# Two steps' products with the values in one run on TensorE, the second maxima group behind a slice of filler

## The chip, the cores and the metric

The kernel runs on one core of one Trainium2 chip. The metric is the device time of one launch in microseconds (us). A kernel is timed several times and the median is taken. Times in the profile come from one profiled execution and count from the first instruction of the program.

## The reference

Two kinds of layer alternate, each with a residual: attention with 16 query heads that share one key and one value head, and a gated feed-forward layer. The pair is applied twice with the same weights.

```python
def _A_ref(x, wq, wk, wv, wo):            # S = 2048, D = 448, H = 16, Dh = 28
    q = (x @ wq).reshape(B, S, H, Dh).transpose(0, 2, 1, 3)
    k = x @ wk
    v = x @ wv
    scores = jnp.einsum("bhqd,bkd->bhqk", q, k) * (Dh ** -0.5)
    p = _softmax(scores, axis=-1)
    o = jnp.einsum("bhqk,bkd->bhqd", p, v)
    return o.transpose(0, 2, 1, 3).reshape(B, S, H * Dh) @ wo

def _B_ref(x, w_gate, w_up, w_down):      # F = 1792
    h = _sigmoid(x @ w_gate) * (x @ w_up)
    return h @ w_down

x = x + _A_ref(_layernorm(x), ...); x = x + _B_ref(_layernorm(x), ...)
x = x + _A_ref(_layernorm(x), ...); x = x + _B_ref(_layernorm(x), ...)
```

## The kernel before, in words

The order of all instructions is written out by the program itself: the tile framework adds semaphores, and what Python emits first stands first in an engine's queue.

**Units and steps.** The 2048 queries are cut into 16 units of 128 rows, the keys into 16 tiles of 128. A unit takes 16 steps, one for each key tile, so a layer has 256 steps. A step has these parts, each with a letter in the order string:

- S, four times: `scores` multiplies one key tile with the queries of four heads (`s`, L508, one full-array fp16 product with 96 rows, 512 columns). ScalarE then writes the exponentials into a tile `P` (L511). The `P` tiles turn through 8 buffers.
- P: `pv` multiplies four `P` tiles with the values (L519), four fp32 products side by side on four column strips of the array, added up over a unit in one PSUM bank `pv`. In the trace an fp32 product has two records, so one step shows 8. `pv` is called one step late: after the four scores of step n stands the product of step n-1 (`PLAG = 1`, list `PQ`).
- M: `group(mx)` runs one group of maxima for the next unit: four products on four row strips (`mx`, L466, 32 rows each), each reduced to a maximum by VectorE (L470, `mp`). With the largest score of each row known ahead, the exponentials need no second pass. `m` is half a group (two products).
- T: `finish()`. When the last group of a unit is done, VectorE joins the maxima (`m`, L485 and L486), and `finish` transposes them on TensorE (`mt`, L491), copies them (`mr`, L493) and has SyncE write them into a row of the next unit's query tile (`QS<-mr`, L494). The scores of that unit read this row.
- X: bookkeeping of the step: side work such as layer norms, loads and the small `kv` products is emitted when it is due (`tick`).
- F: a slice of filler: products of the feed-forward layer (`gp`, `up` at L346, `dn` at L706), of the output projection (`wo`, L615) or of the next queries (`qp`, L346), for as many ns as the rate says. At each slice the put-off evictions of filler are emitted too (`th`, `h` on ScalarE, `th`, `h` on VectorE, L669 to L681).

A pattern holds two steps. `FULL` is taken while the filler left makes over 600 ns a step, `LEAN` otherwise; `LEAN` splits each maxima group into two halves. A unit with filler is one that runs in `FULL`.

```python
while step < U * KT:
    order = FULL if rate > LEANR else LEAN
    for o in order:
        ...
        elif o == "P":
            if len(PQ) > (sn % 4 == 0) * PLAG:
                pv(*PQ.pop(0))
        ...
        else:
            fill.slice(rate * 2 / order.count("F"))
```

**Banks.** One PSUM bank belongs to `pv`. The other seven are one pool that `s`, `mx`, `gp`, `up`, `dn`, `qp`, `wo`, `kv` and `mt` share. Which bank a product gets is fixed when the program is written out, and the product waits for the engine that last reads what the bank held.

Of the kernel before, what the change touches and what calls it, by code (L numbers as in the profile page):

```python
# [8 lines left out]
F32 = mybir.dt.float32  # L9
# [10 lines left out]
def interleaved_layers_kernel(ctx: ExitStack, tc: tile.TileContext, x, wq, wk, wv, wo, wg, wu, wd, out, layers=2):  # L20
# [6 lines left out]
    nc = tc.nc  # L27
# [3 lines left out]
    NT, NB, G, KT, FC = S // 128, S // 512, H // 4, S // 128, F // 128  # L31
    U = NT
    TB, WB, HB = 2, 4, 10
    NBL = NT // TB
    EPS = 1e-5

# [5 lines left out]
    wk1 = ctx.enter_context(tc.tile_pool(name="wk1", bufs=2))  # L42
# [27 lines left out]
    def flush(every=False):  # L70
        todo, pend[:] = pend[:], []
        for i, (due, fn) in enumerate(todo):
            if due > now[0] and not every:
                pend.append((due, fn))
            else:
                fn()
        if every and pend:
            flush(True)
# [331 lines left out]
    def qgen(l, b):  # L410

        XT = XTQ.pop((l, b))
        for g in range(G):
            yield from qproj(l, XT, b, g)
        flush(True)
# [89 lines left out]
    def scores(l, u, kt, g, P):  # L505
        assert ("m", l, u) in stored, (l, u, kt)
        s = psf.tile([128, 512], F32, tag=BANKS["s"], name="s", bufs=NBK[BANKS["s"]])
        nc.tensor.matmul(s, KK[l][0:96, 0, kt * 128:(kt + 1) * 128], QS[l, u][:, g].rearrange("p h n -> p (h n)"),  # L508
                         start=True, stop=True)
        p = wk1.tile([128, 512], F32, tag="P", name="P", bufs=8)  # L510
        nc.scalar.activation(p, s, AF.Exp, scale=esc)  # L511
        P.append(p)

    def pv(l, u, kt, P):
        if kt == 0:
            PVS[l, u] = psv.tile([128, 512], F32, tag="v", name="pv")
        v = PVS[l, u]
        for g in range(4):
            nc.tensor.matmul(v[32 * g:32 * g + 32], VV[l][:, kt], P[g], start=kt == 0, stop=kt == KT - 1,  # L519
                             tile_position=(0, 32 * g))  # L520
        if kt == KT - 1:
            o = wk1.tile([128, 512], F32, name="pvs", bufs=1)
            nc.scalar.copy(o, v)
            PVS[l, u] = o
# [5 lines left out]
    def later(*stages):  # L530

        side.append([stages[0][0], list(stages)])

    def tick():

        for s in list(side):
            s[0] -= 1
            if s[0] <= 0:
                flush()
                fill.run(s[1].pop(0)[1]())  # L540
                if s[1]:
                    s[0] = s[1][0][0]
                else:
                    side.remove(s)

    class Block:
# [8 lines left out]
        def tile(self, u):  # L555
# [84 lines left out]
            def ff():  # L640
                self.fed += 1
                if self.fed == TB:
                    fill.add(self.bulk(), BULK)
                    if b == NBL - 1 and not self.last:
                        fill.add(qgen(l + 1, 1), G * QCH)
# [372 lines left out]
    for b, g in sorted(qnew):  # L1018
        fill.add(qrest(b, g), QCH)

    FULL = "FSFSFSFSTPXMFSFSFSFSTPXM"
    LEAN = "FSFSmFSFSTPXmFSFSmFSFSTPXm"
    PLAG = 1
    LEANR = 600.0
    MORE = (5, 10)
    FIRST = KT * TB + 16
# [2 lines left out]
    for l in range(layers):  # L1029
# [15 lines left out]
        P = []  # L1045
        sn = 0
# [3 lines that stand above are left out]
                u, kt = divmod(step, KT)  # L1050
                if o == "S":
                    su, skt = divmod(sn // 4, KT)
                    if sn < 4 * U * KT:
                        scores(l, su, skt, sn % 4, P)
                        sn += 1
                        if sn % 4 == 0:
                            PQ.append((l, su, skt, P))
                            P = []
# [6 lines left out]
# [3 lines that stand above are left out]
                elif o == "X":  # L1068
# [9 lines left out]
                    tick()  # L1078
                    fed = sum(BLK[l, b].fed == TB for b in range(NBL) if (l, b) in BLK)
                    if fed < NBL - 1:  # L1080
                        rate = fill.left / max(FIRST + TB * KT * fed - step, 1)
# [7 lines left out]
        flush(True)  # L1089
        later(*BLK[l, NBL - 1].tile(U - 1))  # L1090
        if not final:
# [33 lines left out]
```

## Time and profile before

| what | value |
|---|---|
| median of 3 runs | 2327.27 us (2326.44 to 2330.89) |
| the profiled execution | 2331.67 us, span 2329.9 us |
| mean granted TensorE clock | 0.988 |
| TensorE busy | 96% of the span |
| VectorE busy | 70% |
| ScalarE busy | 67% |
| share of the span on TensorE in the chain that ended last | 53% |

The profiled execution is 4.4 us above the median of the runs. In the profile PE is TensorE's matmuls, PEld its weight loads, DVE VectorE, ACT ScalarE, POOL GpSimd, SPq the queue of SyncE, which issues most DMAs. A row of the timeline gives the start in us, the time from the first start to the last end, engine, line, operation, output and inputs, shape, and how many instructions were merged; in brackets stands the idle time of the engine before it and what ended it. Matmul records overlap, since they are pipelined: what a product costs the queue is the distance from its start to the start of the next row, not its own duration.

### The profile page before, as it was taken

The page shows a single profiled execution, that of the slowest core. Times are in us where ns is not written, and L with a number is a line of the kernel's source. Part 1 is how long each engine was busy: PE and PEld are TensorE (multiplying, and loading weights), DVE is VectorE, ACT ScalarE, POOL GpSimd, SP SyncE. Part 2 cuts the span into 40 slices and gives each one's busy share as a digit, 9 for nine tenths or more (in the row PEclk, how much of TensorE's full clock was granted, in tenths as well). Part 3 has the DMA queues.
Part 4 walks back from the last instruction along what each step waited for, and adds up shares of the span by engine and source line. Part 5 has one row for each costly group of instructions (what it writes and reads, how often), then busy time and mean ns, then how long its engine had stood idle before and what let it go on. Part 6 is the DMA issues. An engine that isn't in the chain of part 4 may idle for free.

```text
span 2329.9 us, 41129 instructions
## 1 busy us (share of the span) xinstructions
PE 2246.5 (96%) x15770; PEld 1003.9 (43%) x15770; DVE 1637.6 (70%) x2887; ACT 1552.1 (67%) x2573; POOL 331.4 (14%) x599
## 2 busy tenths in 40 slices
PE   4899999999999999999999999999999999999999
PEld 3312244444444444444562224444444444444456
DVE  5888887777777777773358887767777777777322
ACT  4577886777667677777413877767676767767751
POOL 6345351000110000001101010000000000000010
PEclk9989999999999999999998999999999999999999
DMA  5624552323223232322341112323131313223133
GB/s 145 202 92 125 173 157 71 97 77 95 92 68 101 70 90 75 95 93 80 97 139 53 28 50 93 89 83 87 60 99 59 99 59 99 77 83 95 59 113 118
DMA packets 224693, 217.53 MB, mean 93 GB/s; under 512 B 154656, under 2 KB 185568, under 8 KB 224496
## 3 DMA queue, kind: packets, MB, share of 16 engines
q1 hardware_dynamic: 218784, 199.12, 29.5%
q0 software_dynamic: 3552, 12.12, 1.3%
q10 hardware_dynamic: 2160, 3.67, 0.5%
q8 instruction: 123, 2.02, 0.4%
q14 instruction: 74, 0.61, 0.1%
HBM read 175.37 MB, written 23.59 MB: 85 GB/s over the span
## 4 chain that ended last, share of the span: by engine, by line
PE 53%; DVE 3%; DMA 1%; ACT 1%; issue 1%; POOL 0%; SPq 0%; ACTq 0%; POOLq 0%; DVEq 0%
PE pv L519 12%; PE s L508 11%; PE gp L346 7%; PE dn L706 7%; PE up L346 7%; PE mx L466 5%; DVE mp L470 2%; PE wo L615 2%; PE qp L346 1%; ACT P L511 1%; DMA sums<-rc 0%; PE mt L491 0%; DMA rc<-sums 0%; DVE m L485 0%; DMA sums<-pvs 0%
## 5 line engine op out<-in xcount | busy, mean ns | idle before, releaser
L511 ACT ACTIVATE P<-s,esc 128x512 f32<-128x512 f32 x2048 | 1303.6, 689 | 489.7 <-PE s L508 473.0
L470 DVE TENSOR_REDUCE mp<-mx 128x1 f32<-128x512 f32 x2048 | 1269.2, 683 | 381.5 <-PE mx L466 380.0
L508 PE MATMUL s<-QS,KK 96*128 96x512 f16 x2048 | 747.7, 383 | 19.0 <-ACT P L511 9.5
L346 PEld LDWEIGHTS <-wgu 128*128 128x128 f16 x4928 | 458.6, 97 | 237.0 <-issue 91.5
L519 PE MATMUL pv<-P,VV 128*32 128x512 f32 x4096 | 551.4, 610 | 0.0
L346 PE MATMUL up<-XT,wgu 128*128 128x256 f16 x2464 | 374.6, 272 | 0.0
L346 PE MATMUL gp<-XT,wgu 128*128 128x256 f16 x2464 | 374.2, 273 | 0.2 <-DVE mp L470 0.2
L706 PE MATMUL dn<-WD,h 128*128 128x448 f16 x1344 | 321.4, 352 | 0.0
L466 PE MATMUL mx<-KK,QH 32*128 32x512 f16 x2048 | 255.5, 389 | 13.5 <-DMA QH<-qd 4.0
L466 PEld LDWEIGHTS <-QH 32*128 32x128 f16 x2048 | 62.0, 91 | 462.3 <-issue 457.1
L508 PEld LDWEIGHTS <-KK 96*128 96x128 f16 x2048 | 189.5, 97 | 131.0 <-issue 57.8
L706 PEld LDWEIGHTS <-h 128*128 128x128 f16 x1344 | 124.1, 98 | 137.8 <-issue 24.0
L593 POOL TENSOR_TENSOR lb<-pvs,lb 128x512 f32<-128x512 f32 x32 | 40.7, 1270 | 968.3 <-DMA lb<-sums 812.7
L519 PEld LDWEIGHTS pv<-P,VV 128*32 128x32 f32 x4096 | 81.5, 108 | 185.8 <-issue 174.3
L680 ACT ACTIVATE h<-th 128x512 f16<-128x512 f32 x112 | 70.4, 628 | 84.0 <-DVE th L677 83.8
L677 DVE SCALAR_TENSOR_TENSOR th<-th,up 128x512 f32<-128x512 f32 x112 | 76.1, 680 | 58.8 <-PE up L346 46.2
L681 DVE SCALAR_TENSOR_TENSOR h<-th,h 128x512 f16<-128x512 f32 x112 | 77.9, 695 | 46.8 <-ACT h L680 46.8
L669 ACT ACTIVATE th<-gp,gsc 128x512 f32<-128x512 f32 x112 | 76.9, 687 | 47.9 <-PE gp L346 47.9
L306 POOL TENSOR_SCALAR rs<-mv 128x1 f32<-128x1 f32 (+2 forms) x53 | 12.2, 230 | 640.2 <-DVE mv L301 581.1
L346 PE MATMUL qp<-XT,WQ 128*128 128x512 f16 x352 | 98.8, 392 | 1.0 <-DVE mp L470 0.7
L615 PE MATMUL wo<-WO,oT 128*128 128x448 f16 x384 | 79.4, 357 | 0.2 <-DVE oT L600 0.2
L346 PEld LDWEIGHTS <-WQ 128*128 128x128 f16 x352 | 32.9, 100 | 51.9 <-issue 26.7
(138 smaller groups left out, 803.8 us busy)
## 6 DMA issues: line engine op xcount, KB each, us to landing
wgu<-wgu_d SPq DMA_DIRECT2D x224, 512.0 KB
QS<-qd SPq DMA_DIRECT2D x384, 32.0 KB
lb<-sums SPq DMA_DIRECT2D x128, 64.0 KB
wgu_d<-sgu POOLq DMA_DIRECT2D x14, 512.0 KB, 3.5
qd<-qst POOLq DMA_DIRECT2D x18, 256.0 KB, 2.7
xr<-in_A_x_dram SPq DMA_DIRECT2D x16, 224.0 KB
QH<-qd SPq DMA_DIRECT2D x28, 128.0 KB
x2d<-x SPq DMA_DIRECT2D x16, 224.0 KB
```

The source lines that it names most:

```text
L346: nc.tensor.matmul(ps, a, b, start=n == 0, stop=n == 10)
L466: nc.tensor.matmul(ps[h], qh[32 * h:32 * h + 32, g], KK[l][32 * h:32 * h + 32, 1, kb * 512:(kb + 1) * 512], start=True, stop=True, tile_po ...
L470: nc.vector.tensor_reduce(mp[:, g, h, kb:kb + 1], ps[h], axis=AX.X, op=OP.max)
L508: nc.tensor.matmul(s, KK[l][0:96, 0, kt * 128:(kt + 1) * 128], QS[l, u][:, g].rearrange("p h n -> p (h n)"), start=True, stop=True)
L511: nc.scalar.activation(p, s, AF.Exp, scale=esc)
L519: nc.tensor.matmul(v[32 * g:32 * g + 32], VV[l][:, kt], P[g], start=kt == 0, stop=kt == KT - 1, tile_position=(0, 32 * g))
L615: nc.tensor.matmul(p, v["oT"][:, a, h * 128:(h + 1) * 128], WO[:, c, h], start=n == 0, stop=n == 11)
L669: defer(lambda: nc.scalar.activation(th, gp.rearrange("p j n -> p (j n)"), AF.Tanh, scale=gsc))
L677: nc.vector.scalar_tensor_tensor(t, th, 1.0, up.rearrange("p j n -> p (j n)"), op0=OP.add, op1=OP.mult)
L680: nc.scalar.activation(h[:, 0], t, AF.Copy, scale=2.0 ** -17)
L681: defer(lambda: nc.vector.scalar_tensor_tensor(h[:, 1], t, 2.0 ** -17, h[:, 0], op0=OP.mult, op1=OP.subtract), 1)
L706: nc.tensor.matmul(p, hs[f // 2][:, a, o:o + 128], WD[:, f, c], start=n == 0, stop=n == 3 * FC - 1)
```

## The change

The string `FULL` is written anew. In its first step two `P` stand together, the second step has none; the second step has no `T`; and the second step's `M` stands behind one more slice of filler instead of behind a `P`. So a pattern has nine slices in place of eight, each 8/9 as long. In the steady state three sets of `P` tiles are there when the two `pv` come (those of steps n-2, n-1 and n), so the `P` tiles turn through 12 buffers in place of 8. Room for them is made by a smaller scratch area for the descriptors of GpSimd's DMAs (4096 bytes of each partition; it is the default otherwise).

```diff
     TB, WB, HB = 2, 4, 10
+    PB = 12
...
-        p = wk1.tile([128, 512], F32, tag="P", name="P", bufs=8)
+        p = wk1.tile([128, 512], F32, tag="P", name="P", bufs=PB)
...
-    FULL = "FSFSFSFSTPXMFSFSFSFSTPXM"
+    FULL = "FSFSFSFSTPPXMFSFSFSFSFXM"
     LEAN = "FSFSmFSFSTPXmFSFSmFSFSTPXm"
     PLAG = 1
+
...
-    nc = _bacc.Bacc("TRN2", target_bir_lowering=False, num_devices=1)
+    nc = _bacc.Bacc("TRN2", target_bir_lowering=False, num_devices=1, dynamic_dma_scratch_size=4096)
```

Line numbers behind the first edit are one higher in the changed kernel, and two higher behind the string.

TensorE's order where a unit's maxima are transposed, in the second layer's part where `dn` is the filler. Before, in the second step of a pattern:

```order
L508 MATMUL s<-QS,KK 128x512
L491 LDWEIGHTS m_20722
L491 MATMUL mt<-id_79,m_20722 16x128
L519 MATMUL pv<-P,VV 32x512 x4
L466 LDWEIGHTS QH
L466 MATMUL mx<-KK,QH 128x512
```

Now the same transpose of the same unit, in the first step of a pattern:

```order
L509 MATMUL s<-QS,KK 128x512
L492 LDWEIGHTS m_20721
L492 MATMUL mt<-id_79,m_20721 16x128
L520 MATMUL pv<-P,VV 32x512 x8
L467 LDWEIGHTS QH
L467 MATMUL mx<-KK,QH 128x512
```

The run of products with the values has grown from four to eight, and the transpose has moved four scores products further down.

TensorE's order at a maxima group in the same stretch. Before, every group stands right behind products with the values:

```order
L508 LDWEIGHTS KK
L508 MATMUL s<-QS,KK 128x512
L519 MATMUL pv<-P,VV 32x512 x4
L466 LDWEIGHTS QH
L466 MATMUL mx<-KK,QH 128x512
```

Now the group of the second step, between two slices of filler:

```order
L509 MATMUL s<-QS,KK 128x512
L707 LDWEIGHTS h
L707 MATMUL dn<-WD,h 128x448
...
L467 LDWEIGHTS QH
L467 MATMUL mx<-KK,QH 128x512
...
L707 LDWEIGHTS h
L707 MATMUL dn<-WD,h 128x448
```

In front of the group there is no product with the values any more, but two or three of the filler. Over the whole program the products with the values stand in 508 runs of four and 2 of eight before, and in 94 runs of four and 209 of eight now. Of the maxima groups of four, 369 stood behind products with the values before and 190 do now; 179 more stand behind filler.

## The prediction

> **What bounds the kernel now.** I read the page from the top: engines' shares, the chain that ended last, the costliest groups.
>
> ```profile
> span 2329.9 us, 41129 instructions
> PE 2246.5 (96%) x15770; PEld 1003.9 (43%) x15770; DVE 1637.6 (70%) x2887; ACT 1552.1 (67%) x2573; POOL 331.4 (14%) x599
> L511 ACT ACTIVATE P<-s,esc 128x512 f32<-128x512 f32 x2048 | 1303.6, 689 | 489.7 <-PE s L508 473.0
> L470 DVE TENSOR_REDUCE mp<-mx 128x1 f32<-128x512 f32 x2048 | 1269.2, 683 | 381.5 <-PE mx L466 380.0
> ```
>
> TensorE is busy nearly all the time, and the two engines that empty its banks sit idle for hundreds of us until TensorE gives them something. That is an average, so next the two long stretches of units with filler, by windows, and the group of the products with the values in the second of them.
>
> ```profile
> 350.00:1082.00 732.00, 725.55 (x5256) 329.97 (x5255) 543.10 (x958) 515.36 (x838) 66.30 (x174) 1.00 0.29 84
> 1482.00:2190.00 708.00, 704.40 (x5059) 318.59 (x5057) 517.95 (x886) 498.52 (x797) 44.05 (x99) 1.00 0.27 80
> L519 PE MATMUL pv<-P,VV 128*32 128x512 f32 x1400 | 186.5, 604 | 0.0
> ```
>
> In both, PE (the third number) is busy over 99% and the granted clock is 1.00. 1400 records are 175 steps in 708 us, 4.05 us a step. Here only fewer or shorter occupations of TensorE's queue shorten the kernel, so I read the distances between starts. This is the timeline of TensorE over one step and the start of the next:
>
> ```profile
> 605.22 0.38 PE L508 MATMUL s<-QS,KK 96*128 96x512 f16 x1
> 605.53 1.07 PE L519 MATMUL pv<-P,VV 128*32 128x512 f32 x8
> 606.53 0.40 PE L466 MATMUL mx<-KK,QH 32*128 32x512 f16 x4
> 606.86 0.61 PE L346 MATMUL up<-XT,wgu 128*128 128x256 f16 x4
> 607.30 0.38 PE L508 MATMUL s<-QS,KK 96*128 96x512 f16 x1
> 607.52 0.71 PE L346 MATMUL up<-XT,wgu 128*128 128x256 f16 x5
> ...
> 609.49 0.38 PE L508 MATMUL s<-QS,KK 96*128 96x512 f16 x1
> 609.80 1.06 PE L519 MATMUL pv<-P,VV 128*32 128x512 f32 x8
> 610.80 0.39 PE L466 MATMUL mx<-KK,QH 32*128 32x512 f16 x4
> 611.13 0.72 PE L346 MATMUL gp<-XT,wgu 128*128 128x256 f16 x5
> ```
>
> A scores product takes 0.22 us ahead of filler (607.30 to 607.52), but 0.31 ahead of the products with the values (605.22 to 605.53). These take 1.00, the maxima 0.33. No idle time is shown, so the 0.09 is a price of the change from full array to column strips.
>
> **The change part by part.** I count pairs of steps. 209 runs of eight stand now where 2 were, so 207 pairs are merged.
>
> *Two products in a row.* The trace of before has this at the end of the first layer:
>
> ```profile
> 1131.02 0.38 PE L508 MATMUL s<-QS,KK 96*128 96x512 f16 x1
> 1131.33 1.92 PE L519 MATMUL pv<-P,VV 128*32 128x512 f32 x16
> 1133.19 1.05 PE L346 MATMUL gp<-XT,wgu 128*128 128x256 f16 x8
> ```
>
> Two steps in a row take 1131.33 to 1133.19 = 1.86 us, against 2 x 1.00 apart: 0.14 less. Ahead of them the scores product pays its 0.31 once, and the other one goes back to 0.22: 0.09 less. 207 x 0.14 = 29.0 and 207 x 0.09 = 18.6 us saved.
>
> *The second maxima group behind filler* changes from full array to row strips, which the neighbour `pv` paid for before. Rows for it, the first two inside a layer, the others from between the layers:
>
> ```profile
> 600.17 0.81 PE L346 MATMUL qp<-XT,WQ 128*128 128x512 f16 x3
> 600.82 0.38 PE L508 MATMUL s<-QS,KK 96*128 96x512 f16 x1
> 1232.64 1.46 PE L346 MATMUL qp<-XT,WQ 128*128 128x512 f16 x6
> 1234.03 0.40 PE L466 MATMUL mx<-KK,QH 32*128 32x512 f16 x4
> ```
>
> Three such products take 0.65 ahead of a scores product, 0.217 each; six take 1.39 ahead of maxima, which is 0.09 over 6 x 0.217. 179 groups move behind filler: 179 x 0.09 = 16.1 us lost. The way back, maxima to filler, stays 0.33. The same filler is cut into nine slices instead of eight; a slice has no price of its own in these rows (607.52 follows at 0.22, as inside a row of full-array products), so 0.
>
> The Trainium skill (TensorEngine Tiling (Array Packing), Key Properties) says that a change of the tiling mode drains TensorE and a change of tile alone does not. The trace agrees with 0.09 us at each way in. By the rule alone a pair goes from six changes to five, one 0.09 less, 18.6 us over 207 pairs; by the rows the balance of both paragraphs is 29.0 + 18.6 - 16.1 = 31.5, since the last products of a run also have a longer end.
>
> *The transpose* now stands one step later behind its last maxima group. The waits of TensorE in the two stretches, in order:
>
> ```profile
> PE mt L491 <- DVE m L486: 2.6, 4, 0.7
> PE s L508 <- DVE mp L470: 2.2, 6, 0.4
> PE s L508 <- ACT P L511: 0.7, 3, 0.4
> PE mt L491 <- DVE m L486: 3.0, 11, 0.4
> ```
>
> The 5.6 us on `mt` were a wait for VectorE, which has 4 us more now; I take 5 as saved. Its followers move with it: VectorE's copy `mr`, now behind four more reductions, and SyncE's `QS<-mr`, which keeps its place between the same transfers on that queue. The next unit's first scores product waits for it. That distance was two and a half steps and becomes 1.86 + 0.33 + one step without its product (3.3) + a slice (0.4) = 5.9 us. The nearest row that bounds what is needed is at the start of the second layer:
>
> ```profile
> 1254.68 0.28 PE L491 MATMUL mt<-id,m 128*16 128x128 f16 x1
> 1255.23 0.58 SPq L494 DMA_DIRECT2D QS<-mr  x1
> 1257.96 0.60 PE L508 MATMUL s<-QS,KK 96*128 96x512 f16 x2
> ```
>
> 3.28 us from transpose to scores there, without a wait shown: 2.6 us to spare, so 0. The other end, a delay of up to 1 us at each of the 31 later units, would be 31 us and belongs to no row, so it only widens the range upwards by a little.
>
> *Banks and the two engines that empty them.* The pause on `s` and `mx` during two products is 1.86 instead of 1.00, but the other eight scores products and the second maxima group now come without one. Filler per step is 4.05 - 1.64 - 3 x 0.22 = 1.75 us, a slice 2 x 1.75 / 9 = 0.39. From the first maxima group to the second: 0.33 + 5 x 0.39 + 4 x 0.22 + 0.09 = 3.25 us instead of 4.05. What the engines need:
>
> ```profile
> 1703.88 1.85 ACT L511 ACTIVATE P<-s,esc 128x512 f32<-128x512 f32 x3
> 1706.12 0.39 PE L466 MATMUL mx<-KK,QH 32*128 32x512 f16 x4
> 1706.54 2.48 DVE L470 TENSOR_REDUCE mp<-mx 128x1 f32<-128x512 f32 x4 [0.50 <-PE mx L466]
> 1706.78 0.38 PE L508 MATMUL s<-QS,KK 96*128 96x512 f16 x1
> 1707.20 2.61 ACT L511 ACTIVATE P<-s,esc 128x512 f32<-128x512 f32 x4 [0.31 <-PE s L508]
> 1864.48 0.69 ACT L669 ACTIVATE th<-gp,gsc 128x512 f32<-128x512 f32 x1 [0.87 <-PE gp L346]
> 1865.07 1.26 ACT L511 ACTIVATE P<-s,esc 128x512 f32<-128x512 f32 x2
> ```
>
> VectorE is done with a group 1706.12 to 1709.02 = 2.90 us after its start: 0.35 to spare for the second group, which the four reductions, emitted together, seldom lose. An exponential ends 0.42 + 0.69 = 1.11 us after its scores product starts, and in a queue (1703.88, three in 1.85) one follows each (1.85 - 0.69) / 2 = 0.58 us, while the scores products come each 0.22 + 0.39 = 0.61: ScalarE just keeps pace. A filler activation in between costs it 0.59 (1864.48 to 1865.07). In the changed program's banks, 81 of the groups behind filler reuse the bank of the second scores product in front of them and 96 more that of the third. The third stands 0.22 + 0.39 + 0.22 + 0.39 + 0.09 = 1.31 us ahead, 0.20 to spare without a filler activation. One stands between in 29 groups; these, and about as many scores products right behind the second group, wait perhaps 0.2 us (0.59 less the spare time): some 58 x 0.2 = 12 us, an estimate. Below nothing it cannot go by more than the 2.9 us of scores waits shown. Above, if every one of the 179 groups lost the 0.59 less 0.20, it would be 70. I take 12, nearest to the rows, since the same engines left only 2.9 us of such waits in 1440 us.
>
> *Twelve `P` tiles*: with three sets alive the exponentials of a step still reuse tiles whose product was issued before, so no wait; 0. *The smaller descriptor area*: GpSimd issues the same transfers in the same order, POOL is 14% busy; 0. No row gives it a price.
>
> The sum: -29.0 - 18.6 + 16.1 - 5 + 12 = -24.5 us. Against the profiled execution 2331.7 - 24.5 = 2307.2; the median stands 4.4 lower than that execution, 2327.3 - 24.5 = 2302.8. I say **2303**.
>
> **The rivals.**
>
> *Clean gain.* The waits on banks stay as rare as before: -36.5 us, 2291. For it: idle time on ScalarE and VectorE, spare time in each sum above. Against: ScalarE's 0.58 against 0.61 is no reserve.
>
> *The banks take it all (slower).* In the denser half TensorE runs ahead of ScalarE, and the second maxima group or the scores behind it wait in most pairs. Price: what is left without that term is 36.5 us over 179 groups, so from 0.20 us a group on the change loses. At 0.39 (one filler activation ahead in each) it is 70 us: 2327.3 - 36.5 + 70 = 2361; at 0.26, 2337. For it: the spare 0.20 and 0.35 us are small, and both engines already run at 70 to 74% in these stretches (515.36 of 732 us, 543.10 of 732). Against: only 29 groups have such an activation ahead. The Trainium skill (TensorEngine Tiling (Array Packing), PSUM Bottleneck) speaks for this one: tiling speeds TensorE up, not the emptying of PSUM, which may become the limit. The trace so far agrees only with the 2.9 us above.
>
> *Nothing left.* The products of two steps do not run on as at 1131 us, because inside a unit the second waits for its exponentials or for weights, and only the 0.09 at the scores stays: 18.6 - 16.1 + 5 - 12 is about -5 to +5: 2322 to 2332. Against: the second step's exponentials were issued a step earlier.
>
> **How the numbers follow.** A difference under 0.2% (4.7 us) is about what a measurement of this kernel cannot tell from none. The chances: forecast 0.55, clean gain 0.21, nothing left 0.11, slower by banks 0.13. Faster holds the first two: 0.76; same 0.11; slower 0.13. The low end goes a little below the clean gain, for the rounding of 0.14 and 0.09 (0.005 x 207 x 2 = 2 us): 2289. The high end takes in the case with nothing left up to 2326; beyond lie the slower case and the upper part of that one, together under 0.2.
>
> **What would show it.** In the profile after: runs of x16 on L520 of 1.86 us; 3.99 us a step on average, with maxima groups 3.25 and 4.7 us apart in turn; scores to filler 0.22 at the end of the second step; filler to maxima 0.09 more than filler alone; no wait on `mt`; and a wait of `mx` or `s` for ScalarE of about 12 us in all. The prediction is wrong if those waits are over 40 us, if a run of x16 takes 2.0, or if `s` waits for `QS<-mr`.

## The result and the profile after

The changed kernel takes 2315.72 us (median of 6 runs, 2311.68 to 2318.61) against 2329.01 us before (6 runs): ratio 0.9943, 95% interval 0.9928 to 0.9957, 13.3 us less. In a second session, beside the runs of before on the same chip, it took 2311.3 us against 2331.8, ratio 0.9915 (0.9901 to 0.9929). The profiled execution took 2316.89 us, 14.8 us less than that of before. 24.5 us less were forecast: 2303 us in a range of 2289 to 2326. The time lies in the range, but the gain is 0.54 of the forecast one in the first session and 0.84 in the second.

From the page after, the lines that answer to those of before:

```profile
span 2315.1 us, 41170 instructions
PE 2229.8 (96%) x15770; PEld 1028.4 (44%) x15770; DVE 1637.9 (71%) x2887; ACT 1530.1 (66%) x2573; POOL 330.4 (14%) x599
PE 80%; DVE 7%; ACT 5%; DMA 3%; issue 2%; POOL 2%; SPq 1%; ACTq 0%; DVEq 0%; POOLq 0%
L509 PE MATMUL s<-QS,KK 96*128 96x512 f16 x2048 | 746.5, 383 | 24.6 <-ACT P L512 12.2
L520 PE MATMUL pv<-P,VV 128*32 128x512 f32 x4096 | 508.5, 606 | 0.0
```

The same number of matmuls; the products with the values are busy 42.9 us less (551.4 to 508.5, records overlap), and TensorE is idle ahead of the scores for 24.6 us instead of 19.0. The chain that ended last has 80% of the span on TensorE. The 53% before can't be compared with it: the shares of that chain add up to 59% only, so the profile did not follow it over the whole span.

The two stretches in which the order differs run from the first scores product of a layer's fourth unit to the last of the layer. Windows of before, then of after (start and end, length, then busy time of PE, PEld, DVE, ACT, POOL, the clock, the DMA share, GB/s):

```profile
279.40:1131.00 851.60, 843.03 (x6124) 386.37 (x6123) 610.61 (x1079) 614.76 (x1010) 102.52 (x214) 1.00 0.31 91
1413.20:2242.00 828.80, 824.67 (x5950) 377.88 (x5948) 579.55 (x991) 590.98 (x949) 52.79 (x118) 1.00 0.28 82
```

```profile
280.80:1127.60 846.80, 833.88 (x6122) 398.31 (x6121) 611.11 (x1079) 604.34 (x1009) 102.11 (x214) 1.00 0.31 92
1411.00:2227.10 816.10, 812.81 (x5956) 389.59 (x5955) 579.04 (x991) 579.21 (x950) 52.83 (x118) 1.00 0.28 84
```

4.8 us are gone in the first layer, 12.7 in the second, 17.5 together. A second profile of the changed kernel has 846.6 and 816.0 here, and one of the old order with the new buffers 851.8 and 828.7: these stretches repeat to a few tenths of a us. What lies outside them scatters by several us (652.2 and 646.1 us in the two profiles of the changed kernel), and is where the two sessions differ.

One pair of steps on TensorE in the second layer, after:

```profile
1690.00 0.38 PE L509 MATMUL s<-QS,KK 96*128 96x512 f16 x1
1690.31 1.92 PE L520 MATMUL pv<-P,VV 128*32 128x512 f32 x16
1692.17 0.39 PE L467 MATMUL mx<-KK,QH 32*128 32x512 f16 x4
1692.50 0.50 PE L347 MATMUL up<-XT,wgu 128*128 128x256 f16 x3
...
1694.59 0.38 PE L509 MATMUL s<-QS,KK 96*128 96x512 f16 x1
1694.81 0.49 PE L347 MATMUL gp<-XT,wgu 128*128 128x256 f16 x3
1695.23 0.40 PE L467 MATMUL mx<-KK,QH 32*128 32x512 f16 x4
1695.56 0.50 PE L347 MATMUL gp<-XT,wgu 128*128 128x256 f16 x3
1695.90 0.38 PE L509 MATMUL s<-QS,KK 96*128 96x512 f16 x1
1696.12 0.49 PE L347 MATMUL gp<-XT,wgu 128*128 128x256 f16 x3
1696.96 0.38 PE L509 MATMUL s<-QS,KK 96*128 96x512 f16 x1 [0.36 <-ACT P L512]
```

Every price of the forecast is there: 0.31 ahead of the products, 1.86 for two sets, 0.33 for the first group, 0.22 at the other step's last scores product, 0.42 for three products of filler ahead of the second group (3 x 0.109 + 0.09). The row at 1696.96 is the part that was undersized: a wait behind the second group, here for ScalarE.

### The profile page after: what moved, and what is told of

Same layout as the page of the kernel before. It is cut to its first block, busy times and chain, and to the rows that moved or that the text cites. A ratio compares the mean times of both kernels' runs of the same rounds, so it can differ in the third digit from the quotient of the medians.

```text
span 2315.1 us, 41170 instructions
## 1 busy us (share of the span) xinstructions
PE 2229.8 (96%) x15770; PEld 1028.4 (44%) x15770; DVE 1637.9 (71%) x2887; ACT 1530.1 (66%) x2573; POOL 330.4 (14%) x599
## 3 DMA queue, kind: packets, MB, share of 16 engines
q1 hardware_dynamic: 218784, 199.12, 29.3%
## 4 chain that ended last, share of the span: by engine, by line
PE 80%; DVE 7%; ACT 5%; DMA 3%; issue 2%; POOL 2%; SPq 1%; ACTq 0%; DVEq 0%; POOLq 0%
PE pv L520 19%; PE s L509 17%; PE dn L707 11%; PE up L347 10%; PE gp L347 9%; PE mx L467 7%; DVE mp L471 5%; ACT P L512 3%; PE wo L616 3%; PE qp L347 2%; SPq L431 0%; DMA WD<-in_A_x_dram 0%; DMA XT<-hl 0%; POOL hl L888 0%; DMA wgu<-wgu_d 0%
## 5 line engine op out<-in xcount | busy, mean ns | idle before, releaser
L512 ACT ACTIVATE P<-s,esc 128x512 f32<-128x512 f32 x2048 | 1282.5, 690 | 481.6 <-PE s L509 471.7
L509 PE MATMUL s<-QS,KK 96*128 96x512 f16 x2048 | 746.5, 383 | 24.6 <-ACT P L512 12.2
L520 PE MATMUL pv<-P,VV 128*32 128x512 f32 x4096 | 508.5, 606 | 0.0
L347 PE MATMUL gp<-XT,wgu 128*128 128x256 f16 x2464 | 387.8, 273 | 0.8 <-DVE mp L471 0.7
L347 PE MATMUL up<-XT,wgu 128*128 128x256 f16 x2464 | 384.8, 272 | 1.2 <-ACT P L512 0.5
L707 PE MATMUL dn<-WD,h 128*128 128x448 f16 x1344 | 330.2, 352 | 0.0
L467 PE MATMUL mx<-KK,QH 32*128 32x512 f16 x2048 | 265.3, 389 | 13.8 <-DMA QH<-qd 4.4
L520 PEld LDWEIGHTS pv<-P,VV 128*32 128x32 f32 x4096 | 102.8, 109 | 237.0 <-issue 229.2
L682 DVE SCALAR_TENSOR_TENSOR h<-th,h 128x512 f16<-128x512 f32 x112 | 77.9, 696 | 49.4 <-ACT h L681 49.4
```

Source lines behind the costliest of these rows:

```text
L347: nc.tensor.matmul(ps, a, b, start=n == 0, stop=n == 10)
L467: nc.tensor.matmul(ps[h], qh[32 * h:32 * h + 32, g], KK[l][32 * h:32 * h + 32, 1, kb * 512:(kb + 1) * 512], start=True, stop=True, tile_po ...
L682: defer(lambda: nc.vector.scalar_tensor_tensor(h[:, 1], t, 2.0 ** -17, h[:, 0], op0=OP.mult, op1=OP.subtract), 1)
L707: nc.tensor.matmul(p, hs[f // 2][:, a, o:o + 128], WD[:, f, c], start=n == 0, stop=n == 3 * FC - 1)
```

## Occupation and waits apart

To tell the time for which a product holds TensorE's queue from the time for which it waits, I took for every row of TensorE in these stretches the distance to the start of the next, less what this neighbourhood takes undisturbed (0.109 for a product of 256 columns of filler, 0.189 for `dn` and `wo`, 0.216 for `qp`, 0.22 for scores, 1.00 or 1.86 for products with the values, 0.33 for a group, 0.09 more at a way into strips), and added up what is over 0.015 us. That is the time waited, idle or not. Sums over both stretches, in us, for before, after and the kernels below:

| kernel | length | waits at `mt` | other waits | the rest |
|---|---|---|---|---|
| before | 1680.4 | 7.6 | 20.2 | 1652.6 |
| after | 1662.9 | 0 | 40.2 | 1622.7 |
| transpose alone moved | 1674.1 | 0 | 21.5 | 1652.6 |
| no slice ahead of the second group | 1686.7 | 0.1 | 64.0 | 1622.6 |
| two slices behind it | 1659.0 | 0 | 37.3 | 1621.7 |
| second group one product later | 1752.9 | 41.1 | 90.2 | 1621.6 |
| half reductions, old order | 1661.6 | 0 | 8.7 | 1652.9 |
| half reductions, new order | 1639.3 | 0 | 16.6 | 1622.7 |

The rest is 1652.6 to 1652.9 for the old order and 1621.6 to 1622.7 for the new one, whatever the waits: the double product, with the price of its second group's new place taken off, is worth 30.0 us. The transposes give 7.6. Other waits grow by 20.0, and 35.4 of the 40.2 us after stand at or behind the second group, before the next double product.

Which engine let a waiting product go can be read from the semaphores of the same traces, as far as releasers can be inferred. Of the other waits before, 9.6 us ended with VectorE and 10.7 with ScalarE; after, 25.2 and 15.2. So VectorE has the larger part of the growth, and ScalarE some 4.5 us.

## Experiments

**Buffers and descriptor area alone.** The changed kernel with the old string:

```diff
-    FULL = "FSFSFSFSTPPXMFSFSFSFSFXM"
+    FULL = "FSFSFSFSTPXMFSFSFSFSTPXM"
```

> The old order string with the twelve P tiles and the smaller descriptor area: the change without its order. Theory A (the whole difference is the order: about 31 us less occupation of TensorE's queue and 7 us less waiting for the transposes, of which some 23 us come back as waits for banks behind the second maxima group): ratio to before 1.000, within 0.0015. Theory B (tiles or descriptor area cost something, and that is what ate the gain): 5 to 20 us slower, ratio 1.002 to 1.009.

Measured: 2332.0 against 2330.7 us, ratio 1.0003 (0.9991 to 1.0014). Tiles and descriptor area cost nothing that can be measured; the order makes the whole difference.

**The transpose alone.** The old kernel without the second T:

```diff
-    FULL = "FSFSFSFSTPXMFSFSFSFSTPXM"
+    FULL = "FSFSFSFSTPXMFSFSFSFSPXM"
```

> The old kernel with only the second T of the pattern taken out: the transpose of a unit's maxima stands one step later, the rest is as before. Theory A: the waits of TensorE for the maxima at the transpose (6.8 us in the stretches with filler) go, nothing comes in their place: 2321 to 2324 us, ratio 0.997. Rival: the scores of the next unit wait for the row instead, or the wait moves to another bank: 2327 to 2331.

Measured: 2323.1 us, ratio 0.9969 (0.9956 to 0.9982), as theory A had it. Of the 13 to 20 us of the whole change, about 7 come from a letter that can be taken out without the double product. The windows of this kernel:

```profile
281.20:1130.80 849.60, 843.42 (x6125) 386.02 (x6123) 611.42 (x1079) 614.29 (x1009) 100.53 (x214) 1.00 0.31 92
1409.70:2234.20 824.50, 823.76 (x5950) 377.49 (x5948) 579.46 (x991) 590.44 (x949) 52.62 (x118) 1.00 0.28 83
```

**No slice ahead of the second group.**

```diff
-    FULL = "FSFSFSFSTPPXMFSFSFSFSFXM"
+    FULL = "FSFSFSFSTPPXMFSFSFSFSXM"
```

> The changed kernel, but the second maxima group right behind the fourth scores product of its step, without the slice of filler between (eight slices, each 9/8 as long). Theory A: the group then needs four banks 0.4 us earlier, while the same scores tiles are still read, so it is 5 to 15 us slower than the changed kernel: 2321 to 2331 us, ratio to before 0.996 to 1.001, with the added waits at the maxima group and just behind it. Theory C (the loss comes from cutting the filler into nine shorter slices, so that scores products follow each other too fast for ScalarE): eight slices make it the same or faster, 2308 to 2317 us.

Measured: 2335.3 us, ratio 1.0020 (1.0009 to 1.0032): the double product with the group in the wrong place is slower than the old kernel. Theory A had the direction and too small a size: 5 to 15 us slower than the changed kernel were expected, and the waits alone grew by 23.8 us (40.2 to 64.0). Theory C, that the shorter slices do the harm, falls. The timeline of TensorE in this kernel shows where it waits:

```profile
1694.06 0.38 PE L509 MATMUL s<-QS,KK 96*128 96x512 f16 x1
1694.37 0.49 PE L467 MATMUL mx<-KK,QH 32*128 32x512 f16 x4
1694.79 0.28 PE L347 MATMUL up<-XT,wgu 128*128 128x256 f16 x1
```

The group takes 0.42 instead of 0.33, without a gap: its fourth product starts 0.11 us behind the third, where undisturbed it is 0.004, and waits for its bank while the first ones run.

**Two slices behind the second group.** One slice moved:

```diff
-    FULL = "FSFSFSFSTPPXMFSFSFSFSFXM"
+    FULL = "FFSFSFSSTPPXMFSFSFSFSFXM"
```

> The changed kernel with the same nine slices, but one of them moved: two slices stand behind the second maxima group, and the last two scores products ahead of the double product stand together. Theory A: the scores products behind the second group then find their banks read, and the late pair has the 1.86 us of the double product to be read: the waits fall by 8 to 16 us, 2300 to 2308 us, ratio to before 0.987 to 0.992. Rival: the two scores products together wait for banks themselves, 2316 to 2325.

Measured: 2311.4 us, ratio 0.9915 (0.9898 to 0.9933). The stretches take 3.9 us less than after. I ran it again beside the changed kernel:

> The changed kernel itself, once more, to stand beside the next run on the same chip: ratio to before 0.993 to 0.9955.

> The kernel with two slices behind the second maxima group, once more beside the changed kernel. Theory A: 3 to 8 us faster than the run before it, ratio 0.990 to 0.9925. Rival: the two are the same within their scatter, 0.993 to 0.995.

Measured: 2311.3 us, ratio 0.9915 (0.9901 to 0.9929), and 2310.4 us, ratio 0.9906 (0.9888 to 0.9923). The changed kernel came out faster than its own expectation, 0.993 to 0.9955, by what lies outside the stretches. The stretches repeat (846.6 and 816.0 for the changed kernel, 844.0 and 815.0 for this one), so some 4 us are shown in the trace. In the time of the whole launch they are within the scatter (0.9 us between the medians), and it is not shown to beat the changed kernel. The waits fell by 3, not by 8 to 16.

**More of the same** brought nothing:

```diff
-    FULL = "FSFSFSFSTPPXMFSFSFSFSFXM"
+    FULL = "FFSFSFSSTPPXMFSFSFSFSFFXM"   # ten slices
+    FULL = "FFSFSFSSTPPXMFSFSFSSFFXM"    # both steps end with two scores products
+    FULL = "FFFSFSSSTPPXMFSFSFSFSFXM"    # three slices behind
```

> The kernel with two slices behind the second maxima group (2311 us) with one slice more ahead of it, ten slices of 0.35 us. Theory A: the group stands 0.3 us later behind its scores products and 0.15 us later behind the first group, which VectorE and ScalarE both need: 2303 to 2309 us. Rival: slices of 0.35 bring scores products 0.57 us apart, faster than ScalarE's 0.58, and the waits come back at the scores: 2312 to 2320 us.

> The changed kernel with nine slices, two behind the second maxima group and two ahead of it: the last two scores products of each step stand together. Theory A (the waits behind the second group come from banks of scores products and maxima read too late; time between the group and its neighbours is what helps): against the kernel with two slices behind it (2311 us, ratio 0.9915) the group keeps its distance to the third scores product and the next scores product stands 0.39 us later; 2 to 8 us faster, ratio 0.988 to 0.991. Rival: the pair ahead of the group is read by ScalarE one after the other just when the group needs banks, so the group itself waits: slower than 0.9915, up to 0.997.

> The changed kernel with three of the nine slices behind the second maxima group and the last three scores products ahead of the double product together. Theory A: the first scores product behind the group finds its bank read in nearly every pair, so that the waits there fall by another 2 to 5 us against two slices (ratio 0.9915): 0.989 to 0.991. Rival: three scores products in a row need three free banks at once behind the group's four, and wait for VectorE and ScalarE: 0.993 to 1.000.

Measured: 2312.4 us, ratio 0.9918 (0.9903 to 0.9934); 2314.5 us, 0.9929 (0.9916 to 0.9942); 2320.9 us, 0.9962 (0.9950 to 0.9974). The rival's range holds each time, for the first kernel just at its edge, but the first two can't be told from the kernel with two slices behind (2311.4 us): their stretches take 1659.6 and 1659.8 us where that one takes 1659.0. Only the third is clearly slower. There the first maxima group, behind the double product, waits for banks for 13.5 us over the two stretches, where it is 0.7 in the changed kernel and 5.5 with two slices behind: more scores products stand close together ahead of it, and room made at one place is taken from another. In the second kernel the rival's reason did not come true: the second group waits less (5.7 us, not 10.0), and the pair of scores products ahead of it waits instead (6.7 us, not 0.8).

**The second group one scores product later.**

```diff
-    FULL = "FSFSFSFSTPPXMFSFSFSFSFXM"
+    FULL = "FSFMSFSFSTPPXMFSFSFSFSFX"
```

> The changed kernel with the second maxima group moved into the next step, behind its first scores product and a slice, so that the two groups stand about 4.2 and 3.7 us apart instead of 3.25 and 4.7. Theory A1: VectorE has done with a group whenever the next comes, the waits fall by 8 to 15 us, 2301 to 2308 us. Theory A2: the group still stands in a run of eight scores products without a pause, ScalarE is as late as before, and the waits only move: 2312 to 2320 us.

Measured: 2404.9 us, ratio 1.0325 (1.0308 to 1.0341). Both theories missed. The waits of TensorE in the second layer's stretch:

```profile
PE mt L492 <- DVE m L487: 19.4, 12, 2.0
PE s L509 <- ACT P L512: 13.1, 27, 0.8
PE s L509 <- DVE x L621: 2.8, 12, 0.2
...
```

The last group of a unit now stands in the same step as its transpose, which waits 1.6 us each time in these rows for the join of the maxima, 41 us in both stretches by the table; and the other waits, most of them at and behind this group, are more, not less (90 us). So this order did not help. It is no clean test of a more even distance between the groups, since a scores product now stands directly behind the group, without a slice between, and since the transposes are in the way; neither was tried apart.

**Half the reductions**, in the new and the old order:

```diff
-nc.vector.tensor_reduce(mp[:, g, h, kb:kb + 1], ps[h], axis=AX.X, op=OP.max)
+nc.vector.tensor_reduce(mp[:, g, h, kb:kb + 1], ps[h][:, 0:256], axis=AX.X, op=OP.max)
```

> The changed kernel, but VectorE reduces only the first 256 of the 512 columns of each maxima product (the maxima of the other keys are left out), so that a group is read in well under 2.9 us. To be read against the next run, which does the same to the old kernel. Theory A1 (waits behind the second group come mostly from VectorE being late with the maxima): most of the 20 us of VectorE's waits in the stretches with filler go, 2296 to 2304 us, 23 to 32 us faster than the next run. Theory A2 (they come mostly from ScalarE's exponentials, which lack the pause): 5 us at most go, 2309 to 2316 us.

> The old kernel with the same halved reductions (maxima of the second 256 columns left out). Both theories: the waits at the transposes and the few scores waits for VectorE, together some 12 us, go: 2316 to 2322 us, ratio to before 0.995 to 0.997.

Measured: 2265.6 us, ratio 0.9722 (0.9707 to 0.9737), and 2284.7 us, ratio 0.9803 (0.9786 to 0.9820). Both gain far more than expected: the old order gains 46 us, 19 of them in the stretches and the rest mostly in the units without filler, where VectorE is waited for as well. The new order is 19.1 us faster than the old one, less than the 23 to 32 of theory A1. What the pair was for can be read: in the stretches the new order is 22.3 us faster than the old one, where it was 17.5. The windows of the new order:

```profile
264.80:1095.70 830.90, 824.92 (x6123) 398.58 (x6122) 414.88 (x1079) 602.86 (x1011) 101.98 (x214) 1.00 0.32 94
1367.40:2175.80 808.40, 807.73 (x5955) 389.10 (x5954) 381.87 (x991) 578.93 (x950) 52.62 (x118) 1.00 0.28 85
```

VectorE's busy time falls from 611 to 415 us in the first stretch, and the other waits the change adds from 20.0 to 7.9 us. So some 12 of the 20 us hang on the length of VectorE's reductions. What the run leaves, 7.9 us, stays with ScalarE or with VectorE's other work. No run parts these two.

## Where VectorE is late

The timeline of all engines in the first layer, after, at a second group:

```profile
427.72 0.40 PE L467 MATMUL mx<-KK,QH 32*128 32x512 f16 x4
427.88 0.36 ACT L372 ACTIVATE ktl<-kv 128x224 f16<-128x224 f32 x1
428.05 0.39 PE L509 MATMUL s<-QS,KK 96*128 96x512 f16 x1
...
428.12 0.21 ACT L373 ACTIVATE VV<-kv 128x28 f32<-128x28 f32 x1
428.28 0.38 PE L347 MATMUL up<-XT,wgu 128*128 128x256 f16 x2
428.36 0.19 DVE L374 SCALAR_TENSOR_TENSOR ktl<-kv,ktl 128x28 f16<-128x28 f32 x1 [0.96 <-ACT VV L373]
428.46 0.24 DVE L577 RECIPROCAL rc<-rc 128x16 f32<-128x16 f32 x1
...
428.62 2.42 DVE L471 TENSOR_REDUCE mp<-mx 128x1 f32<-128x512 f32 x4
...
429.30 0.38 PE L509 MATMUL s<-QS,KK 96*128 96x512 f16 x1 [0.43 <-DVE mp L471]
```

VectorE is not busy when the group comes: it is idle from 427.40 to 428.36, 0.96 us. At the head of its queue stands a small instruction of the side work, which waits for ScalarE, and the four reductions stand behind it. They start 0.90 us after the group instead of 0.42, and the second scores product behind the group, 1.58 us after it, finds the bank of the first reduction still taken. The same wait, 0.60 us, recurs in this layer every second unit (at 700.4 and 831.1 us, for example).

Counted over both stretches, 62 of the 187 second groups see their first reduction start more than 0.5 us after the group, and 29.4 of the 35 us waited at and behind second groups belong to these 62. In 22 of them the instructions just ahead are those of these rows (L374, L577) or the filler's eviction `h` (L682): VectorE stands idle until ScalarE is done, and 16.5 us belong to them. In 33 others it is a layer norm's instruction (L302, L323), with 10.7 us. Late reductions are not new: before, 58 of 376 groups were as late, but cost 13.9 us together, about half as much each. In the new order the second group no longer has the products with the values ahead of it, 1.00 us in which the other engines could catch up. That this is why a late reduction now costs twice as much is likely, but no run shows it apart.

ScalarE has its share too. In windows inside the two stretches (350 to 1075 us, then 1470 to 2175) the view of TensorE's waits has these as the largest; the last line is the only one of its window:

```profile
PE s L509 <- DVE mp L471: 4.6, 14, 0.4
PE s L509 <- ACT P L512: 1.5, 5, 0.3
...
PE s L509 <- ACT P L512: 1.8, 5, 0.4
```

The side work for the next layer's keys and their layer norms is there in the first layer alone. Other waits grow by 14.4 us in the first stretch (14.8 to 29.3) and by 5.6 in the second (5.4 to 11.0), while the layers gained 4.8 and 12.7 us. That the side work makes this difference is argued from the rows; no run leaves it out.

## Why the prediction was right, point by point

- *What bounds it*: right. In the stretches the length less the waits fell by 30.0 us, and it stayed at its value for each order in every kernel of the table.
- *Two products in a row* and *the second group behind filler*: 29.0 + 18.6 - 16.1 = 31.5 forecast, 30.0 measured, from one pair of rows at the layer's end and one between the layers. The double product is 1.86 us in its place.
- *The transpose*: 5 us forecast, 7.6 measured in the stretches, and shown alone by a run. The distance to the next scores, forecast 5.9 us, is 5.4 to 6.9 in nearly all units, and no scores product waits for the row.
- *Banks*: the term that was mis-sized, and the reason why the gain fell short. 12 us forecast, 20.0 measured. The place was right (behind the second group), the engine only in part: I looked at ScalarE's pace, which added some 4.5 us, and gave VectorE 0.35 us to spare, "which the four reductions, emitted together, seldom lose". They lose it to what stands ahead of them in VectorE's queue, in 62 of 187 second groups. I took the duration of a group's reading from a group that VectorE was ready for, and never looked what stands ahead of the reductions in the changed order.
- The 2.9 us of waits from which I reasoned were idle time alone, read from the view of waits. By the distances the old kernel waited 20.2 us beside the transposes, in windows that are somewhat longer. So they were no ground for taking this term small. That the time still lies in the range is in part luck: the transposes gave 2.6 us more than forecast, and the range reached far up for another case, the one with nothing left.
- *The sign at 40 us*: ScalarE was said to make about 12 us of waits, with over 40 as a sign of being wrong. ScalarE makes 15.2 us, all engines together 40.2, and 20.2 of these were there before. Runs of x16 take 1.86 us, and the groups stand 3.17 and then 4.7 to 5.0 us apart (medians; 3.25 and 4.7 were said).
- *Tiles and descriptor area*: 0 forecast, shown by a run.
- By the rule on changes of tiling mode (the Trainium skill, TensorEngine Tiling (Array Packing), Key Properties) alone it would have been 18.6 us in place of 31.5; the runs give 30.0.
- The price named for the rival in which the banks take it all was "From 0.20 us a group on the change loses". Measured was 40.2 - 20.2 = 20.0 us over 179 groups, 0.11 each, and (64.0 - 20.2) / 179 = 0.24 where the slice ahead of the group is missing, which did lose. The Trainium skill (TensorEngine Tiling (Array Packing), PSUM Bottleneck) warns that tiling does not speed up the emptying of PSUM, which may become the limit. The runs agree in part: the waits are for banks, but the engine that was late in many of them stood idle.
- The sum of the measured terms: -30.0 - 7.6 + 20.0 = -17.6 us, against -17.5 in the length of the stretches. The whole launch gained 13.3 and 20.5 us in the two sessions; the difference lies outside the stretches, where the change has no term.

## What to carry to other kernels

Where an engine is busy 99% of a stretch, read the distance from start to start for each neighbourhood: one instance of the new neighbourhood somewhere in the old trace priced the time on the queue within 5% here (31.5 us forecast, 30.0 measured). It does not price the waits. A reordering that takes pauses away also takes away the time in which the other engines catch up, so for each group that now comes sooner look at the queue of the engine that must read it: what stands ahead of it there, and what that waits for. And take a change apart letter by letter: of the 37.6 us that were saved before the new waits took 20.0 back, 7.6 came from a transpose that had only been moved along.

## What was not expected of the hardware

An fp32 set of four products on column strips runs on into the next set on the same strips at 1.86 us for two, against 1.00 us each where maxima or filler follow: the end of a run has 0.14 us that is paid once. And a TensorE wait need not show as idle time: of the 40.2 us waited in the two stretches after, the view of waits has 13.4 us. A scores product's record lasts 0.38 us where the next product may start after 0.22, so the matmul before is still counted as busy while the next one waits for its bank.
